# Attention and a maxout projection: token blocks by parity, 64x64 tiles for the last queries, transposes by DMA

## The chip, the cores and the metric

The kernel runs on one core of a Trainium2 chip. The metric is the device time of one execution in microseconds. The kernel before takes 380.43 us, the median of three runs (380.34 to 380.91). A profiled execution of it spans 377.6 us from its first to its last instruction.

Engines are named as in the profile: PE is TensorE (matmuls), PEld its weight loads, DVE is VectorE, ACT is ScalarE, POOL is GpSimd, SP is SyncE. PSUM is the memory that matmuls write, eight banks; one bank holds 512 fp32 columns on 128 partitions.

## The reference

Softmax attention with one added to the denominator, for 8 batches of 12 heads of 448 tokens and 64 dimensions, then a projection with the maximum of three matrices, then an output matrix. Inputs and output are fp32.

```python
# q, k, v: (8, 12, 448, 64)
scores = scale * np.matmul(q, k.transpose(0, 1, 3, 2))      # scale = 1 / sqrt(64)
m = np.max(scores, axis=-1, keepdims=True)
e = np.exp(scores - m)
attn = e / (np.sum(e, axis=-1, keepdims=True) + np.exp(-m) + 1e-09)
x = matmul(attn, v)                                         # heads side by side: (3584, 768)
h = np.maximum(np.maximum(x @ w1, x @ w2), x @ w3)          # w1, w2, w3: (768, 768)
out = h @ w_out                                             # (3584, 768)
```

Without the shift by the maximum the weight is exp(s) / (sum of exp(s) + 1), which is what both kernels compute, in fp16 with fp32 sums.

## The kernel before

The heads are taken in 24 groups of four (8 batches, three groups each). Tokens are split into 4 chunks of 112. A group has four visits; in each, scores of two chunks for a pair of heads go to PSUM, ScalarE takes exponentials, and between the visits TensorE works off pieces of the projections of the batch before. All loads cast from fp32 to fp16 and are issued by GpSimd.

```python
SC = 112; NCH = 4; GH = 4           # chunk, chunks, heads in a group
ps1 = tile_pool(bufs=4, PSUM)       # one bank each: transposes, sums, projections
ps2 = tile_pool(bufs=2, PSUM)       # two banks each: scores

# transpose_pair: per pair of heads, K and Q in 4 chunks each
nc.tensor.transpose(out=trT[:, n, ts(c, SC)], in_=t16[:, c, :, :], identity=ident16[0:SC, 0:SC])
nc.vector.tensor_copy(out=qkT, in_=trT.rearrange("p n s -> p (n s)"))

# scores_visit: keys of a chunk as rows, two heads in the two halves of the array
nc.tensor.matmul(out=stp[:, hh, 0:S], lhsT=qkT[hh*D : hh*D + D, c*SC : c*SC + 128],
                 rhs=qkT[hh*D : hh*D + D, S : 2*S], start=True, stop=True)
nc.scalar.activation(out=st["eT"][:, 2*pr : 2*pr + 2, c, :], in_=stp[0:SC, :, 0:S],
                     func=AF.Exp, scale=scale)

# av_group: three column-tiled sums, four heads in four strips of 32 columns
for c in range(NCH):
    for hh in range(GH):
        nc.tensor.matmul(out=bank[32*hh : 32*hh + 32, 0:S], lhsT=weights(hh, c),
                         rhs=eT[:, hh, c, :], start=(c == 0), stop=(c == NCH - 1))
# weights: ones (the denominator), then the even and the odd columns of V
nc.scalar.activation(out=lnd, in_=den[:, 0:S], func=AF.Ln, bias=one_b)
nc.scalar.activation(out=rb, in_=lnd, func=AF.Exp, bias=ln_lam, scale=-1.0)
nc.vector.tensor_tensor(out=xT[b][:, 2*g + hf, :], in0=num[:, 0:S], in1=rb, op=ALU.mult)

# up_piece: 6 matmuls of 448 columns, then a copy or a maximum into hT
# out_piece: 6 matmuls of 384 columns, scaled into o_sb; a stored tile has 768 columns
```

In the last steps, the sums of the last group are followed by all pieces of the last batch.

Of the kernel before, what the change touches and what calls it, by code (L numbers as in the profile page):

```python
# [21 lines left out]
def kernel(  # L22
# [16 lines left out]
    SC = 112  # L39
    NCH = S // SC  # L40
    NDC = DM // 128
    NFC = DFF // 128
    GH = 4
    NG = H // GH
    scale = 1.0 / math.sqrt(D)

    tabs = list(get_activation_tables(nc.m.arch).keys())
# [10 lines left out]
    cpool = ctx.enter_context(tc.tile_pool(name="const", bufs=1))  # L58
    ld_pool = ctx.enter_context(tc.tile_pool(name="ld", bufs=5))
    p16_pool = ctx.enter_context(tc.tile_pool(name="p16", bufs=2))  # L60
    att_pool = ctx.enter_context(tc.tile_pool(name="att", bufs=4))
    e_pool = ctx.enter_context(tc.tile_pool(name="e", bufs=2))
    small = ctx.enter_context(tc.tile_pool(name="small", bufs=2))
    xt_pool = ctx.enter_context(tc.tile_pool(name="xt", bufs=2))
    ht_pool = ctx.enter_context(tc.tile_pool(name="ht", bufs=2))
    out_pool = ctx.enter_context(tc.tile_pool(name="outp", bufs=3))

    ps1 = ctx.enter_context(tc.tile_pool(name="ps1", bufs=4, space=bass.MemoryType.PSUM))
    ps2 = ctx.enter_context(tc.tile_pool(name="ps2", bufs=2, space=bass.MemoryType.PSUM))

    ctx.enter_context(tc.manual_schedule())

    groups = [(b, g) for b in range(B) for g in range(NG)]
    raw = {}

    def load_group(i, which="qkv", step=GH):
        b, g = groups[i]
        tiles = raw.setdefault(i, {})
        for name in which:
            tiles[name] = ld_pool.tile(  # L80
                [SC, GH, NCH, D], MMDT, tag="ld_" + name, name="ld_" + name
            )
        for h0 in range(0, GH, step):
            for name in which:
                src = {"q": q, "k": k, "v": v}[name][b].rearrange(
                    "(g h) (p c) d -> g p h (c d)", g=NG, c=NCH
                )[g]
                nc.gpsimd.dma_start(  # L88
                    out=tiles[name][:, h0 : h0 + step].rearrange("p h c d -> p h (c d)"),
                    in_=src[:, h0 : h0 + step],  # L90
                )

    load_group(0, "qk", 2)
    ident16 = cpool.tile([128, 128], MMDT, name="ident16")
    make_identity(nc, ident16)
    load_group(1, "qk")
    load_group(0, "v")
    load_group(1, "v")
    load_group(2)
    ones16 = cpool.tile([SC, 32], MMDT, name="ones16")  # L100
    nc.vector.memset(ones16, 1.0)
    one_b = cpool.tile([128, 1], FP32, name="one_b")
    nc.vector.memset(one_b, 1.0)

    ln_lam = cpool.tile([128, 1], FP32, name="ln_lam")
    nc.vector.memset(ln_lam, math.log(LAMBDA))

    w_sb = [cpool.tile([128, NDC, DFF], MMDT, name=f"w{i}") for i in range(4)]
    wout_sb = w_sb[3]

    def load_weight(i):
        w = (moe_w1, moe_w2, moe_w3, moe_w_out)[i]
        for g in range(NG):
            if i < 3:
                src = w.rearrange("(g p hf) f -> g p hf f", g=NG, hf=2)[g]
            else:
                src = w.rearrange("(g hf p) f -> g p hf f", g=NG, hf=2)[g]
            nc.gpsimd.dma_start(out=w_sb[i][:, 2 * g : 2 * g + 2, :], in_=src)


    state = {}

    def pair_qk(i):
        qf, kf = raw[i].pop("q"), raw[i].pop("k")
        qk16 = []
        for pr in range(GH // 2):
            q16 = p16_pool.tile([SC, NCH, 2, D], MMDT, tag=f"q16_{pr}", name=f"q16_{pr}")
            k16 = p16_pool.tile([SC, NCH, 2, D], MMDT, tag=f"k16_{pr}", name=f"k16_{pr}")
            nc.vector.tensor_copy(
                out=k16, in_=kf[:, 2 * pr : 2 * pr + 2].rearrange("p h c d -> p c h d")  # L130
            )
            nc.vector.tensor_copy(
                out=q16, in_=qf[:, 2 * pr : 2 * pr + 2].rearrange("p h c d -> p c h d")
            )
            qk16.append((q16, k16))
        state[i] = {"qk16": qk16, "qkT": []}

    def transpose_pair(i, pr):
        st = state[i]
        q16, k16 = st["qk16"][pr]  # L140
        trT = ps1.tile([128, 2, S], MMDT, tag="bank1", name="trT")
        for n, t16 in enumerate((k16, q16)):
            for c in range(NCH):
                nc.tensor.transpose(  # L144
                    out=trT[:, n, ts(c, SC)], in_=t16[:, c, :, :],
                    identity=ident16[0:SC, 0:SC],
                )
        qkT = att_pool.tile([2 * D, 2 * S], MMDT, tag="qkT", name="qkT")
        nc.vector.tensor_copy(out=qkT, in_=trT.rearrange("p n s -> p (n s)"))  # L149
        st["qkT"].append(qkT)  # L150

    def scores_visit(i, pr, cs):
        st = state[i]
        if "eT" not in st:
            st["eT"] = e_pool.tile([SC, GH, NCH, S], MMDT, tag="eT", name="eT")
        qkT = st["qkT"][pr]
        stps = []
        for c in cs:
            stp = ps2.tile([128, 2, 512], FP32, tag="bank2", name="stp")
            for hh in range(2):  # L160
                nc.tensor.matmul(  # L161
                    out=stp[:, hh, 0:S],
                    lhsT=qkT[hh * D : hh * D + D, c * SC : c * SC + 128],
                    rhs=qkT[hh * D : hh * D + D, S : 2 * S],
                    start=True,
                    stop=True,
                )
            stps.append(stp)
        for c, stp in zip(cs, stps):
            nc.scalar.activation(  # L170
                out=st["eT"][:, 2 * pr : 2 * pr + 2, c, :],
                in_=stp[0:SC, :, 0:S],
                func=AF.Exp,
                scale=scale,
            )

    xT = {}

    def av_group(i):
        b, g = groups[i]  # L180
        st = state.pop(i)
        eT, v16 = st["eT"], raw[i].pop("v")
        if g == 0:
            xT[b] = xt_pool.tile([128, NDC, S], MMDT, tag="xT", name="xT")

        def col_tiled(weights):
            bank = ps1.tile([128, 512], FP32, tag="bank1", name="av")
            for c in range(NCH):
                for hh in range(GH):
                    nc.tensor.matmul(  # L190
                        out=bank[32 * hh : 32 * hh + 32, 0:S],
                        lhsT=weights(hh, c),
                        rhs=eT[:, hh, c, :],
                        start=(c == 0),
                        stop=(c == NCH - 1),
                    )
            return bank

        den = col_tiled(lambda hh, c: ones16[:, :])
        lnd = small.tile([128, S], FP32, tag="lnd", name="lnd")  # L200
        nc.scalar.activation(out=lnd, in_=den[:, 0:S], func=AF.Ln, bias=one_b)  # L201
        rb = small.tile([128, S], FP32, tag="rb", name="rb")
        nc.scalar.activation(out=rb, in_=lnd, func=AF.Exp, bias=ln_lam, scale=-1.0)  # L203
        for hf in range(2):
            num = col_tiled(lambda hh, c: v16[:, hh, c, hf::2])
            nc.vector.tensor_tensor(  # L206
                out=xT[b][:, 2 * g + hf, :], in0=num[:, 0:S], in1=rb, op=ALU.mult
            )

# [4 lines left out]
    def up_piece(b, fc, i):  # L214
        if b % 2 == 0 and fc == 0 and i == 0:
            hT[b // 2] = ht_pool.tile([128, NFC, 2 * S], MMDT, tag="hT", name="hT")
        dst = hT[b // 2][:, fc, (b % 2) * S : (b % 2) * S + S]
        p_i = ps1.tile([128, 512], FP32, tag="bank1", name="p_i")
        for dc in range(NDC):
            nc.tensor.matmul(  # L220
                out=p_i[:, 0:S],
                lhsT=w_sb[i][:, dc, ts(fc, 128)],
                rhs=xT[b][:, dc, :],
                start=(dc == 0),
                stop=(dc == NDC - 1),
            )
        if i == 0:
            nc.vector.tensor_copy(out=dst, in_=p_i[:, 0:S])  # L228
        else:
            nc.vector.tensor_tensor(out=dst, in0=dst, in1=p_i[:, 0:S], op=ALU.max)  # L230

    NH = 2
    NW = DM // NH

    def out_piece(bp, t, nh):
# [33 lines left out]
    def add_pieces(b):  # L269
        order = [(fc, i) for fc in range(NFC) for i in range(3)]  # L270
        if b == 0:
            order = [(fc, i) for i in range(3) for fc in range(NFC)]
# [98 lines left out]
```

The softmax here doesn't subtract the row's maximum and nothing guards it: scores larger than these inputs give would overflow.

## Time and profile before

| what | value |
|---|---|
| time, median of 3 | 380.43 us |
| span of the profiled execution | 377.6 us |
| granted TensorE clock, mean | 0.999 |
| `p_i` (up projection), share of the chain that ended last | 43.4% |
| `op_ps` (output projection) | 15.0% |
| `av` (sums) | 11.0% |
| `stp` (scores) | 10.0% |
| `trT` (transposes) | 4.2% |
| loads of weights, K and Q | 8.9% |

Busy time is given by engine, with the share of the span. Rows of 40 digits cut the span into 40 equal slices; a digit is the busy share in tenths. In a table by stage the columns are: the stage, its length, then busy time and number of instructions of PE, PEld, DVE, ACT and POOL, then the granted clock, the DMA share and GB/s. The chain that ended last is followed back from the last instruction, at each step to what released it. In a timeline, what stands in brackets is how long the engine was idle before, and what released it.

### The profile page before, as it was taken

The page shows a single profiled execution, that of the slowest core. Times are in us where ns is not written, and L with a number is a line of the kernel's source. Part 1 is how long each engine was busy: PE and PEld are TensorE (multiplying, and loading weights), DVE is VectorE, ACT ScalarE, POOL GpSimd, SP SyncE. Part 2 cuts the span into 40 slices and gives each one's busy share as a digit, 9 for nine tenths or more (in the row PEclk, how much of TensorE's full clock was granted, in tenths as well). Part 3 has the DMA queues.
Part 4 walks back from the last instruction along what each step waited for, and adds up shares of the span by engine and source line. Part 5 has one row for each costly group of instructions (what it writes and reads, how often), then busy time and mean ns, then how long its engine had stood idle before and what let it go on. Part 6 is the DMA issues. An engine that isn't in the chain of part 4 may idle for free.

```text
span 377.6 us, 7320 instructions
## 1 busy us (share of the span) xinstructions
PE 358.3 (95%) x3120; PEld 172.0 (46%) x3120; DVE 194.7 (52%) x395; ACT 194.5 (52%) x241; POOL 59.4 (16%) x92
## 2 busy tenths in 40 slices
PE   2777999999999999999999999999999999999995
PEld 1233444544445444454445544454444554445552
DVE  2233545545546546546546555455465465445553
ACT  1879464663655655555555645546555554552000
POOL 8533450220210201202202202202000000000000
PEclk9999999999999999999999999999999999999999
DMA  7999998555508625455236555077010410013005
GB/s 92 185 208 206 204 196 121 73 136 68 73 2 151 111 54 75 60 139 75 32 43 89 126 101 73 6 128 141 2 26 0 128 43 0 2 32 95 2 0 168
DMA packets 40064, 32.71 MB, mean 87 GB/s; under 512 B 2272, under 2 KB 35296, under 8 KB 40032
## 3 DMA queue, kind: packets, MB, share of 16 engines
q0 software_dynamic: 35552, 21.24, 40.8%
q1 hardware_dynamic: 4480, 11.01, 9.8%
q8 instruction: 24, 0.39, 0.5%
q14 instruction: 8, 0.07, 0.0%
HBM read 42.47 MB, written 11.01 MB: 142 GB/s over the span
## 4 chain that ended last, share of the span: by engine, by line
PE 84%; DMA 9%; ACT 2%; POOL 2%; DVE 1%; issue 1%; DVEq 0%; POOLq 0%
PE p_i L220 43%; PE op_ps L241 15%; PE av L190 11%; PE stp L161 10%; PE trT L144 4%; DMA w_123<-in_moe_w_dram 3%; DMA ld_k<-in_k_dram 3%; DMA ld_q<-in_q_dram 2%; DVE xT L206 1%; ACT eT L170 1%; ACT rb L203 1%; ACT lnd L201 1%; POOL ld_q L88 1%; POOL ld_k L88 1%; POOL ld_v L88 0%
## 5 line engine op out<-in xcount | busy, mean ns | idle before, releaser
L170 ACT ACTIVATE eT<-stp 112x896 f16<-112x896 f32 x192 | 164.9, 916 | 145.1 <-PE stp L161 145.1
L230 DVE TENSOR_TENSOR hT<-hT,p_i 128x448 f16<-128x448 f16 x96 | 59.4, 619 | 45.5 <-PE p_i L220 45.1
L206 DVE TENSOR_TENSOR xT<-av,rb 128x448 f16<-128x448 f32 x48 | 27.8, 619 | 70.8 <-ACT rb L203 64.7
L220 PE MATMUL p_i<-xT,w_122 128*128 128x448 f16 x288 | 63.0, 353 | 0.4
L220 PE MATMUL p_i<-xT,w_123 128*128 128x448 f16 x288 | 62.4, 353 | 0.0
L220 PE MATMUL p_i<-xT,w_124 128*128 128x448 f16 x288 | 62.2, 353 | 0.0
L161 PE MATMUL stp<-qkT 64*128 64x448 f16 x384 | 56.3, 364 | 4.9 <-ACT eT L170 4.8
L241 PE MATMUL op_ps<-w_125,hT 128*128 128x384 f16 x336 | 59.5, 326 | 0.0
L88 POOL DMA_DIRECT2D ld_v<-in_v_dram x24 | 16.8, 702 | 192.3 <-PE av L190 126.3
L248 DVE TENSOR_SCALAR o_sb<-op_ps 128x384 f32<-128x384 f32 x56 | 31.2, 557 | 28.5 <-PE op_ps L241 28.4
L241 PEld LDWEIGHTS <-hT 128*128 128x128 f16 x336 | 30.9, 98 | 24.8 <-issue 6.3
L190 PE MATMUL av<-eT,ld_v 112*32 112x448 f16 x768 | 41.8, 361 | 0.0
L228 DVE CAST hT<-p_i 128x448 f16<-128x448 f32 x48 | 29.7, 620 | 19.9 <-PE p_i L220 19.9
L220 PEld LDWEIGHTS <-w_123 128*128 128x128 f16 x288 | 25.9, 98 | 29.6 <-issue 9.2
L220 PEld LDWEIGHTS <-w_124 128*128 128x128 f16 x288 | 26.0, 98 | 28.7 <-issue 7.8
L220 PEld LDWEIGHTS <-w_122 128*128 128x128 f16 x288 | 26.1, 98 | 27.8 <-issue 7.0
L149 DVE COPY qkT<-trT 128x896 f16<-128x896 f16 x48 | 29.5, 615 | 3.1 <-PE trT L144 3.0
L161 PEld LDWEIGHTS <-qkT 64*128 64x128 f16 x384 | 12.0, 94 | 40.9 <-issue 40.3
L190 PEld LDWEIGHTS <-ld_v 112*32 112x32 f16 x768 | 21.0, 99 | 16.8 <-issue 1.7
L190 PE MATMUL av<-eT,ones_116 112*32 112x448 f16 x384 | 23.3, 364 | 0.0
L88 POOL DMA_DIRECT2D ld_q<-in_q_dram x25 | 17.7, 709 | 6.9 <-DMA w_124<-in_moe_w_dram 1.5
L88 POOL DMA_DIRECT2D ld_k<-in_k_dram x25 | 17.6, 703 | 4.4 <-DMA w_123<-in_moe_w_dram 1.1
(305 smaller groups left out, 142.1 us busy)
## 6 DMA issues: line engine op xcount, KB each, us to landing
ld_v<-in_v_dram POOLq DMA_DIRECT2D x24, 224.0 KB, 4.0
ld_q<-in_q_dram POOLq DMA_DIRECT2D x23, 224.0 KB, 4.9
ld_k<-in_k_dram POOLq DMA_DIRECT2D x23, 224.0 KB, 5.9
out_dram<-o_sb SPq DMA_DIRECT2D x8, 336.0 KB, 2.8
out_dram<-o_sb SPq DMA_DIRECT2D x8, 288.0 KB, 2.7
out_dram<-o_sb SPq DMA_DIRECT2D x8, 240.0 KB, 2.8
out_dram<-o_sb SPq DMA_DIRECT2D x8, 192.0 KB, 2.7
w_122<-in_moe_w_dram POOLq DMA_DIRECT2D x3, 384.0 KB, 10.7
```

Of the source, the lines that this page charges most:

```text
L88: nc.gpsimd.dma_start(out=tiles[name][:, h0 : h0 + step].rearrange("p h c d -> p h (c d)"), in_=src[:, h0 : h0 + step],)
L144: nc.tensor.transpose(out=trT[:, n, ts(c, SC)], in_=t16[:, c, :, :], identity=ident16[0:SC, 0:SC],)
L149: nc.vector.tensor_copy(out=qkT, in_=trT.rearrange("p n s -> p (n s)"))
L161: nc.tensor.matmul(out=stp[:, hh, 0:S], lhsT=qkT[hh * D : hh * D + D, c * SC : c * SC + 128], rhs=qkT[hh * D : hh * D + D, S : 2 * S], sta ...
L170: nc.scalar.activation(out=st["eT"][:, 2 * pr : 2 * pr + 2, c, :], in_=stp[0:SC, :, 0:S], func=AF.Exp, scale=scale,)
L190: nc.tensor.matmul(out=bank[32 * hh : 32 * hh + 32, 0:S], lhsT=weights(hh, c), rhs=eT[:, hh, c, :], start=(c == 0), stop=(c == NCH - 1),)
L206: nc.vector.tensor_tensor(out=xT[b][:, 2 * g + hf, :], in0=num[:, 0:S], in1=rb, op=ALU.mult)
L220: nc.tensor.matmul(out=p_i[:, 0:S], lhsT=w_sb[i][:, dc, ts(fc, 128)], rhs=xT[b][:, dc, :], start=(dc == 0), stop=(dc == NDC - 1),)
L228: nc.vector.tensor_copy(out=dst, in_=p_i[:, 0:S])
L230: nc.vector.tensor_tensor(out=dst, in0=dst, in1=p_i[:, 0:S], op=ALU.max)
L241: nc.tensor.matmul(out=op_ps[:, 0:NW], lhsT=hT[bp][:, fc, ts(t, 128)], rhs=wout_sb[:, fc, ts(nh, NW)], start=(fc == 0), stop=(fc == NFC - 1),)
L248: nc.vector.tensor_scalar(out=o_sb[:, ts(nh, NW)], in0=op_ps[:, 0:NW], scalar1=1.0 / LAMBDA, scalar2=None, op0=ALU.mult,)
```

## The change

It joins several changes.

- **Tokens in blocks of 64 by parity.** A partition now holds 7 tokens of a head, so the 448 tokens of a head are 7 blocks of 64, one for each residue. The transposed Q and K of two neighbouring tokens stand in the two halves of the partitions. The scores are 64x64 tiles, four at a time: two row halves (the parity), two column halves (two blocks of keys).
- **Sums turned round.** The exponentials are now the weights and V is what moves, with a 65th column of 1/256 that gives the denominator. The result has queries as rows; it is normalised on VectorE and then transposed for the projections.
- **The last 64 queries as 64x64 tiles from group 3 on.** Seven blocks are three pairs and one left over. Instead of whole matmuls in which half of the rows are empty, the last block is summed in four 64x64 tiles in two PSUM banks, whose halves are added afterwards.
- **Transposes by DMA.** From group 7 on Q and K, and from group 6 on the attention result, are transposed by DMA, not by TensorE. GpSimd copies Q into the half of the other parity.
- **A start in two parts.** The first pair of heads comes uncast over two hardware queues, TensorE runs matmuls on zeros while it waits, and groups 0 to 2 are done for the last 192 queries first, then for the first 256, with the projections of the 192 between.
- **PSUM.** Three tiles of two banks for scores and sums, two of one bank for projections and transposes.
- **The end.** The last output tile is stored as 640 and 128 columns, over two queues.

The core of the diff; cuts are marked.

```diff
-    SC = 112
-    NCH = S // SC
+    HP = 64
+    T = S // HP
+    NE, NO = 4 * HP, 3 * HP
...
+    PE_QK = 7
+    PE_X = 2
+    LAST = 3
...
-    ps1 = ctx.enter_context(tc.tile_pool(name="ps1", bufs=4, space=bass.MemoryType.PSUM))
-    ps2 = ctx.enter_context(tc.tile_pool(name="ps2", bufs=2, space=bass.MemoryType.PSUM))
+    ps_s = ctx.enter_context(tc.tile_pool(name="ps_s", bufs=3, space=bass.MemoryType.PSUM))
+    ps_b = ctx.enter_context(tc.tile_pool(name="ps_b", bufs=2, space=bass.MemoryType.PSUM))
...
+    for nm, src, eng in (("k", k, nc.sync), ("q", q, nc.scalar)):
+        first[nm] = cpool.tile([P, T, D], FP32, name="first_" + nm)
+        pair = src[0, 0:2].rearrange("h (x t) d -> (h x) (t d)", t=T)
+        eng.dma_start(out=first[nm].rearrange("x t d -> x (t d)"), in_=pair)
...
+    def transpose_dma(i):
...
+        for dst, nm, o in ((QT[i], "q", 4), (KT[i], "k", 0)):
+            nc.sync.dma_start_transpose(
+                out=dst[:, o * 128 : (o + T) * 128].rearrange("p (j x) -> p j x", x=P),
+                in_=raw[i][nm][:, 1 : NB + 1].rearrange("x t d -> x (t d)"),
+            )
...
+    def scores(i, ej, units, part="EO"):
...
+                        nc.tensor.matmul(
+                            out=stp[half * HP : half * HP + HP, par, j * qn : (j + 1) * qn],
+                            lhsT=k_block(i, pr, h2, x[half]),
+                            rhs=q_cols(i, pr, h2, par, part),
+                            start=True,
+                            stop=True,
+                        )
...
+    def av_tail(i, ej, pr, ws=(0, 1, 2, 3)):
...    # the seventh block of keys, as 64x64 tiles
+    def av_last(i, ej, pr):
...    # the seventh block of queries, as 64x64 tiles
+    def av_main(i, ej, pr, ws=(0, 1, 2, 3), last=False):
+        for hh in range(2):
+            for j, w in enumerate(ws):
+                for c, x in enumerate((X1, X3, X2)):
+                    o = e_col(where[pr, hh, x], w)
+                    nc.tensor.matmul(
+                        out=ps[:, hh, j * D1 : (j + 1) * D1],
+                        lhsT=eF[:, o : o + 128],
+                        rhs=vx[:, 2 * pr + hh, (x[0]), 0:D1],
+                        start=False,
+                        stop=(c == 2),
...
+        nc.vector.reciprocal(out=rb, in_=rb)
+        nc.vector.tensor_tensor(
+            out=xn[i][:, pr, ws[0] : ws[0] + nw].rearrange("p j h d -> p h j d"),
...
-        lnd = small.tile([128, S], FP32, tag="lnd", name="lnd")
-        nc.scalar.activation(out=lnd, in_=den[:, 0:S], func=AF.Ln, bias=one_b)
...
+    def av(i, ej, pr, part):
+        if i >= LAST:
+            av_tail(i, ej, pr, (0, 1, 2))
+            av_last(i, ej, pr)
+            return av_main(i, ej, pr, (0, 1, 2), True)
+        av_tail(i, ej, pr, PW[part])
+        av_main(i, ej, pr, PW[part])
...
+            cuts = [(0, NW, None), (NW, NW, (sy, sy))]
+            if b == B - 1 and t == 6:
+                cuts = [(0, NW, None), (NW, 256, (sy, sc)), (NW + 256, 128, (sy, sc))]
...
+    visits = ((0, 1), (2, 3), (4, 5, 6))
...
+            scores(i, ej, units)
...
+            if vi < 2:
+                finish = av(i - 1, pj, vi, "E" if first else "EO")
...
+            if finish:
+                one()
+                finish()
+            if vi == 1 and i > 3 * PE_X:
+                x_transpose_dma(i - 1)
...
+            fill(per)
```

## The prediction, made before the changed kernel ran

> **What bounds the kernel now.** I read the page first, then four stages of the span, then the chain that ended last within one stretch of steady work, then the end of the timeline. The page's first two parts:
>
> ```profile
> span 377.6 us, 7320 instructions
> PE 358.3 (95%) x3120; PEld 172.0 (46%) x3120; DVE 194.7 (52%) x395; ACT 194.5 (52%) x241; POOL 59.4 (16%) x92
> ...
> PE   2777999999999999999999999999999999999995
> ...
> ACT  1879464663655655555555645546555554552000
> ...
> DMA  7999998555508625455236555077010410013005
> ```
>
> TensorE is busy in every slice but the first four and the last; no other engine is above 52%. The busy time per stage (PE, PEld, DVE, ACT, POOL) says the same:
>
> ```profile
> 0.00:38.73 38.73, 24.91 (x260) 11.11 (x260) 10.96 (x31) 26.51 (x33) 20.29 (x36) 1.00 1.11 173
> 38.73:47.44 8.71, 8.39 (x63) 3.90 (x60) 5.79 (x13) 3.72 (x6) 3.88 (x6) 1.00 1.26 204
> 47.44:342.78 295.34, 294.97 (x2618) 141.30 (x2622) 161.19 (x324) 162.95 (x202) 35.27 (x51) 1.00 0.45 75
> ```
>
> From 47 to 343 us TensorE never stops, at the full clock (1.00). So time there is the sum of issue times on TensorE, and these I take from the chain, where each piece is the time until the next piece begins (start, length, what), and not from the mean of a matmul on the page (353 ns), in which pipelined matmuls overlap. One group of four heads:
>
> ```profile
> 196.47 0.48 PE stp L161 x4
> 196.95 2.38 PE av L190 x48
> 199.33 1.24 PE p_i L220 x6
> 200.57 0.48 PE stp L161 x4
> 201.06 1.24 PE p_i L220 x6
> 202.30 0.40 PE trT L144 x8
> 202.70 0.98 PE op_ps L241 x6
> 203.67 0.48 PE stp L161 x4
> 204.16 1.08 PE op_ps L241 x6
> ```
>
> What the reader is to see: six output matmuls of 384 columns behind a transpose take 0.98 us (162.5 ns each); the same six behind a score tile take 1.08. In the last batch the six up-projection matmuls of 448 columns start every 1.137 us, 189.5 ns each; behind `stp` or `av` they take 1.24. Two pairs of `stp` should be 2 x 189.5 = 379 ns and take 484. So every step from tiled matmuls to whole ones or back costs about 0.105 us. Eight transposes of 112 columns take 0.40: 49.5 ns each. The sums (`av`, 48 matmuls, four at a time) are 12 x 189.5 = 2.27 us plus one step.
>
> Check: a group needs 36 x 189.5 + 14 x 162.5 + 8 x 189.5 (score pairs) + 12 x 189.5 + 16 x 49.5 = 13.68 us, plus nine steps = 14.63. The sums of two neighbouring groups begin at 109.13, 123.76 and 138.12: 14.6 and 14.4. The model holds.
>
> The end: the last scaling on VectorE, after which only the store's flight to 377.6 us is left, 4.1 us behind it.
>
> ```profile
> 372.95 0.56 DVE L248 TENSOR_SCALAR o_sb<-op_ps 128x384 f32<-128x384 f32 x1 [0.42 <-PE op_ps L241]
> ```
>
> **What the Trainium skill says.** (1) "TensorE: Matmul & The Clock Gate", section "Back-to-back issue gap", gives N/2.4 + 2.5 ns for a warm matmul of N columns: 189.2 for 448, 162.5 for 384, 49.2 for 112. The trace agrees (189.5, 162.5, 49.5). The same section's 81 ns for a stream of 128-column matmuls with weight loads does not fit: here 112 columns with a new weight load each take 49.5, and I go by that. (2) "TensorEngine Tiling (Array Packing)", section "Key Properties": changing the tiling mode drains the engine. The trace agrees, 0.105 us each way. (3) The same page, section "PSUM Bottleneck": tiling speeds up TensorE and not the emptying of PSUM; the trace of before shows no such wait (4.8 us on `stp` in all, early). (4) "DMA: Bandwidth & Descriptors", section "Latency and other measured facts": about 261 GB/s for a transposing DMA. No transfer in this trace transposes.
>
> **The change part by part.** The counts are from the order of both built programs.
>
> *Up and out projections.* Before 864 x 189.5 = 163.7 us. After 756 of 448 columns, 108 of 256 (109.2 ns by the formula) and 108 of 192 (82.5): 143.3 + 11.8 + 8.9 = 164.0. Output 336 x 162.5 = 54.6 both times. **+0.3**.
>
> *Scores.* Before 384/2 x 189.5 = 36.4. After, 64x64 tiles, four at a time, keys in blocks of 64 so that no row of a 128-row tile is empty (112 of 128 before): 588/4 x 189.5 + 84/4 x 109.2 + 84/4 x 82.5 = 31.9. **-4.5**.
>
> *Sums with V.* Before 54.6 us, a third of it the denominator from `ones`. Now the exponentials are the weights and V with a column of constants moves, 65 columns: 900 whole matmuls and 1188 of 64x64. This is the step I know least. By the formula 65 columns are 29.6 ns; a matmul with its own load of 128 weights has been seen at 49.5 and not below. I choose 36 ns, and 45 ns for four 64x64 tiles: 900 x 36 + 297 x 45 = 32.4 + 13.4 = 45.8. **-8.8**.
>
> *Transposes.* Before 384 x 49.5 = 19.0. After, 119 for Q and K of groups 0 to 6 and 48 for the attention result of groups 0 to 5, 128 columns (55.8 ns): 9.3. The rest goes through DMA, three transfers of about 0.25 MB in a group, 0.72 MB in some 13 us; at the page's rate an estimate of 2.8 us, hidden, as DMA is 0.45 busy in the steady stage. **-9.7**.
>
> *Steps between modes.* Before 24 groups x 0.95 = 22.8. After, scores and the 64x64 sums stand in one tiled stretch; the order shows 82 stretches, two steps each: 82 x 0.21 = 17.2. **-5.6**.
>
> *ScalarE and VectorE.* 24 x 7 exponentials of 896 at 0.86 us (164.9/192) are 6.0 us a group for 6.9 before, and Ln and Exp of 448 columns (1.3 us a group) go; small copies come. VectorE loses qkT copies and the four K and Q copies and gains a normalisation of about 1 us per pair of heads. Both stay near half busy; nothing for the sum.
>
> *Start.* Up to 38.73 us TensorE issues only three groups' attention, 3 x (4 x 0.484 + 2.38 + 0.8) = 15.4 us, so 23 us are lost, to loads and to exponentials (ACT 26.5 busy of 38.7). The change loads the first pair of heads uncast over the hardware queues, scores only 192 of 448 queries in all three groups first, and up-projects these. Exponentials are then 3/7 of 3 x 6.0, some 8 us instead of 25. But the first weight stands behind 4.3 MB of Q, K and V: 6.7 MB with itself. The page's first slices moved 92 and 185 GB/s of 2-byte data, which is twice that read: 5.2 MB by 18.9 us, 9.2 MB by 28.3, so the weight is there at about 22 us and the second at 30. TensorE has about 10 us of work before 22 us; 12 lost, and 4 in the stretch up to the third weight. 16 for 23.3. **-7.3**.
>
> *End.* The last piece is 128 columns instead of 384: the scaling takes perhaps a third of 0.56, the store as long as before. **-0.7**.
>
> *New stall.* Projections now have two PSUM banks where four served all. In the pure projection stretch of the last batch VectorE ends with a bank about 0.13 us before TensorE would come round to it (0.62 us copy, 1.137 us per piece). Each normalisation that VectorE does between makes TensorE wait a little: 42 of them at 0.1 us. **+4**.
>
> Sum: 0.3 - 4.5 - 8.8 - 9.7 - 5.6 - 7.3 - 0.7 + 4 = -32.3, from 380.4 us: **348 us**.
>
> **The rivals.** *Weight loads bound the sums.* At 49.5 ns a matmul and 60 ns a round of tiles the sums cost 62.4 instead of 45.8 and the time is 365. For it: no matmul with its own weights below 49.5 ns in the trace. Against: that is what its 112 columns need anyway, so the load was hidden. *The sums run at the column rate.* 29.6 and 30 ns: 35.6 us, the time is 338. *PSUM's two banks become the bound.* If VectorE is late by 0.5 us at each of 63 visits, 31 instead of 4: 375. For it is the thin 0.13 us; against it, VectorE at 55%, and that the program puts a projection piece ahead of the late part of each normalisation. *Transfers come late.* If transposing DMAs or the GpSimd queue (copies and five issues of 0.7 us a group) need more than a group's 13 us, TensorE waits in each group; 2 us in 17 groups gives 382. Against: they are issued one to two groups ahead. *The start gains nothing*, as the same bytes come first: 355.
>
> **Range and chances.** The sums give -10 to +17, the start +-7, the banks -4 to +15, rarely all on one side; the removed transposes, mode steps and score columns (20 us) are counts times measured times and hardly in doubt. 334 to 362 should hold it 8 times in 10. Faster by over 2% (below 372.8) 0.96, within 2% 0.03, slower 0.01: only late transfers or banks at their worst reach there.
>
> **What would show it.** In the chain of the changed kernel, between two groups after group 7: about 13.0 us apart, with no transposes; `stp` x28 at 0.19 us per four; the `avp` pieces about 0.95 us per pair of heads (0.8 or 1.3 for the first two rivals). Among TensorE's waits, those on VectorE's `hT` or `o_sb` for the banks, 4 us in all; none on a transposing DMA. First `p_i` near 22 us. Wrong would be: TensorE below 90% busy in the steady stage, or its clock under 1.00.

## The result and the profile after

The changed kernel takes 341.09 us, the median of four runs (340.13 to 342.21), beside 380.38 us before: a ratio of 0.898, 95% interval 0.895 to 0.901. The prediction was 348 with 334 to 362. Its profiled execution spans 339.7 us, 37.9 less than before.

The page's first two parts of the changed kernel:

```profile
span 339.7 us, 10313 instructions
PE 327.5 (96%) x4340; PEld 196.0 (58%) x4340; DVE 201.4 (59%) x539; ACT 187.8 (55%) x307; POOL 146.4 (43%) x260
...
PE   7899999999999999999999999999999999999993
...
DMA  8999999299697999969996889989991640114016
```

TensorE still bounds the kernel, and it is busy at 90% or more from the third slice on, where it was the fifth. GpSimd went from 16% to 43% (87 us more, 46.7 of them copies of Q), and the DMA engines are busy to the end of the steady part (the transposes), but nothing waits there for long. A stage of steady work, columns as before:

```profile
100.00:200.00 100.00, 100.00 (x1327) 56.27 (x1329) 60.99 (x165) 62.54 (x107) 46.96 (x85) 1.00 1.02 160
```

The chain that ended last, in one group of the changed kernel (start, length, what):

```profile
191.85 0.50 PE stp L304 x8
192.36 0.09 PE avp L344 x12
192.45 0.13 PE avp L361 x14
192.58 0.67 PE avp L388 x18
...
196.59 3.41 PE p_i L490 x18
199.99 0.69 PE stp L304 x12
200.69 3.51 PE p_i L490 x18
```

What is left out are twelve output matmuls and a second visit like the first; no transposes are left in the chain. Eight score tiles take 0.50 us: two rounds of four at 189.5 ns and one step. Eighteen up-projection matmuls take 3.51 us behind scores, and 3.41 behind the sums; the step between the modes then lies between the 64x64 sums (L344, L361) and the whole ones (L388), so 0.67 us is a step and 18 x 31.4 ns. The 26 tiles in 0.22 us are 34 ns for four. From group 11 to group 20 the first scores move from 128.12 to 242.03 us, 12.66 us a group; in the kernel before, the same groups took 14.67 (152.26 to 284.29 us).

The end: the last scaling is short, but the store behind it ends 4.8 us after it (4.1 before).

```profile
334.59 0.29 DVE o_sb L521
```

### The profile page after: what moved, and what is told of

It is laid out like the page before. It is cut to its first block, busy times and chain, and to the rows that moved or that the text cites. A ratio compares the mean times of both kernels' runs of the same rounds, so it can differ in the third digit from the quotient of the medians.

```text
span 339.7 us, 10313 instructions
## 1 busy us (share of the span) xinstructions
PE 327.5 (96%) x4340; PEld 196.0 (58%) x4340; DVE 201.4 (59%) x539; ACT 187.8 (55%) x307; POOL 146.4 (43%) x260
## 4 chain that ended last, share of the span: by engine, by line
PE 90%; DVE 4%; ACT 4%; issue 1%; ACTq 0%
PE p_i L490 49%; PE op_ps L514 15%; PE stp L304 11%; PE avp L388 9%; ACT e L324 3%; PE avp L344 2%; PE avp L361 2%; PE warm L175 1%; DVE xn L404 1%; DVE QT L190 1%; DVE hT L501 1%; PE trT L213 1%; DVE rb L401 0%; PE xtp L450 0%; PE trT L229 0%
## 5 line engine op out<-in xcount | busy, mean ns | idle before, releaser
L490 PE MATMUL p_i<-xT,w 128*128 128x448 f16 (+2 forms) x972 | 173.4, 332 | 2.0 <-DVE hT L501 1.0
L324 ACT ACTIVATE e<-stp 128x896 f16<-128x896 f32 (+4 forms) x171 | 143.5, 900 | 49.5 <-PE stp L304 49.1
L490 PEld LDWEIGHTS <-w 128*128 128x128 f16 x972 | 90.1, 98 | 71.2 <-issue 8.0
L249 POOL COPY QT<-QT 64x384 f16<-64x384 f16 (+1 forms) x84 | 46.7, 556 | 96.4 <-DMA QT<-ld_q 60.7
L501 DVE TENSOR_TENSOR hT<-hT,p_i 128x448 f16<-128x448 f16 (+2 forms) x96 | 59.7, 621 | 36.9 <-PE p_i L490 36.8
L514 PE MATMUL op_ps<-w,hT 128*128 128x384 f16 (+2 forms) x342 | 58.7, 323 | 0.0
L304 PE MATMUL stp<-QT,KT 64*64 64x448 f16 (+2 forms) x756 | 48.7, 340 | 2.3 <-ACT e L324 0.9
L521 DVE TENSOR_SCALAR o_sb<-op_ps 128x384 f32<-128x384 f32 (+2 forms) x57 | 31.2, 547 | 16.5 <-PE op_ps L514 15.9
L388 PE MATMUL avp<-vx,e 128*128 128x65 f16 x900 | 37.5, 194 | 0.0
L388 PEld LDWEIGHTS <-e 128*128 128x128 f16 x900 | 30.9, 97 | 2.3
L344 PEld LDWEIGHTS <-e 64*64 64x64 f16 x600 | 13.5, 107 | 9.1 <-issue 2.9
```

The source lines that it names most:

```text
L249: eng.tensor_copy(out=t[d0 : d0 + HP, o * 128 : (o + n) * 128], in_=t[s0 : s0 + HP, a * 128 : (a + n) * 128],)
L304: nc.tensor.matmul(out=stp[half * HP : half * HP + HP, par, j * qn : (j + 1) * qn], lhsT=k_block(i, pr, h2, x[half]), rhs=q_cols(i, pr, h2 ...
L324: nc.scalar.activation(out=dst, in_=src, func=AF.Exp, scale=scale)
L388: nc.tensor.matmul(out=ps[:, hh, j * D1 : (j + 1) * D1], lhsT=eF[:, o : o + 128], rhs=vx[:, 2 * pr + hh, (x[0]), 0:D1], start=False, stop= ...
L490: nc.tensor.matmul(out=p_i[:, j * qn : (j + 1) * qn], lhsT=w_sb[i][:, dc, ts(fc, 128)], rhs=xT[b][:, dc, q0 : q0 + qn], start=(dc == 0), s ...
L501: nc.vector.tensor_tensor(out=dst, in0=dst, in1=src, op=ALU.max)
```

## The experiments

Theory: the time is the sum of TensorE's issue times and of what it loses at the start and the end; each part of the change is worth the matmuls, the transposes and the mode steps that it takes away. Rivals: weight loads bound the sums; the two PSUM banks of the projections are the limit; most of the gain is the start.

Short diffs; "+" is the experiment. Times are medians, ratios are to the kernel before.

### The disputed cost by itself: the whole sums twice

```diff
-                for c, x in enumerate((X1, X3, X2)):
+                for c, x in enumerate((X1, X3, X2, X1, X3, X2)):
...
-                        stop=(c == 2),
+                        stop=(c == 5),
```

The output is of sums in which all but the seventh block of keys counts twice (the last 64 queries, which go through the tiles from group 3 on, keep their sums there).

> The 900 whole matmuls of 65 columns of the sums are done twice (the output is then of doubled sums), which measures the disputed cost by itself. The trace of the changed kernel has 18 of them in 0.67 us with one mode step of 0.105: 31.4 ns each, so +28 us, 369 us. The prediction's 36 ns would give +32 (373); a bound by the load of 128 weights, 49.5 ns, +45 (386).

Measured: 369.3 us, ratio 0.976 (0.969 to 0.982), which is 28.2 more than the changed kernel. In its chain:

```profile
195.47 1.23 PE avp L388 x36
```

36 take 1.23 us where 18 took 0.67: 31.1 ns each. The total says the same, 28.2 us / 900 = 31.3 ns, though its interval is some 5 us wide. A matmul of 65 columns with a new load of 128 x 128 weights costs its columns and hardly more. The bound by weight loads is out.

### One part alone in the kernel before: DMA transposes

```diff
+        if i >= 3:
+            qkT = att_pool.tile([2 * D, 2 * S], MMDT, tag="qkT", name="qkT")
+            for n, t16 in enumerate((k16, q16)):
+                nc.sync.dma_start_transpose(
+                    out=qkT[:, n * S : n * S + S].rearrange("p (c x) -> p c x", x=SC),
+                    in_=t16.rearrange("p c h d -> p (c h d)"),
+                )
...
```

> One part of the change alone, in the kernel before: Q and K of groups 3 to 23 are transposed by DMA (two transfers per pair of heads), which takes 336 of its 384 TensorE transposes of 49.5 ns and 42 copies out of PSUM away. Theory (parts add up): 380.4 - 16.6 = 364 us. Rival (the part pays only together with the others, or the transfers come late): above 372.

Measured: 372.5 us, ratio 0.981 (0.978 to 0.984): above the 372 of the rival, and less than half of the gain of the theory. The chain in the start:

```profile
33.51 8.34 DMA qkT<-q
...
41.98 0.93 PE stp L170 x4
42.91 4.60 PE av L199 x48
```

The first transposes, of group 3, are issued while the weights still fill the DMA engines, and TensorE waits 6.7 us for one that takes 8.3. Behind the wait it runs at half rate for a while: four scores in 0.93 us, not 0.48, 48 sums in 4.60, not 2.38. In the steady part the theory holds: the same visit two batches later (175.64 and 258.78 us) gives 13.86 us a group, 0.77 less than before, for 16 x 49.5 ns = 0.79. The sums of group 3 begin 7.6 us later than in the kernel before (58.92, not 51.36), those of the last group 7.1 us earlier (334.70, not 341.83). So the part is worth its count, and half was lost because it began too early.

### The same mistake in the changed kernel: DMA transposes earlier

```diff
-    PE_QK = 7
+    PE_QK = 5
-    PE_X = 2
+    PE_X = 1
```

> DMA transposes from group 5 on for Q and K and from group 3 on for the attention result, instead of 7 and 6: 52 TensorE transposes of 55.8 ns fewer (2.9 us), and 7 copies out of the projections' two banks. Theory (sum): 338 us; with the banks as the limit it is more, 335. Rival (loads of the weights still fill the DMA engines up to 60 us, so the transposes come late): slower than 341, with TensorE waiting on transposing DMAs.

Measured: 345.3 us, the median of four executions (two more, at 348.8 and 349.2 us, count as a slower state), ratio 0.908 (0.904 to 0.913). The rival holds. Its chain:

```profile
45.90 12.76 DMA KT<-ld_k
...
58.70 0.96 PE stp L304 x8
```

A transpose of group 5 needs 12.8 us (the median of this kernel is 5.6 for K), the scores wait 5.3 us for it, and behind the wait eight score tiles take 0.96 us instead of 0.50. The 2.9 us of fewer transposes are lost and 4 more. So groups 7 and 6 as first ones are no arbitrary choice; later ones were not tried.

### All transposes back on TensorE

```diff
-    PE_QK = 7
+    PE_QK = NI
-    PE_X = 2
+    PE_X = B
```

> The changed kernel with every transpose but the last group's back on TensorE (238 more for Q and K, 136 more for the attention result, 374 x 55.8 ns = 20.9 us). Theory (time is the sum of TensorE's issue times): 341 + 21 = 362 us, TensorE waits as few as now. Rival (the projections' two PSUM banks are the limit): every transpose tile takes one of them and a copy of 0.6 to 0.9 us on VectorE or ScalarE, some 51 more tiles; then 370 us or more, with waits of TensorE on those copies. Rival (transposes were hidden): under 350.

Measured: 389.3 us, ratio 1.026 (1.022 to 1.029), slower than the kernel before. TensorE's waits (who waited for whom, us in total, times, longest):

```profile
PE p_i L490 <- ACT QT L188: 8.4, 11, 0.8
PE p_i L490 <- DVE hT L499: 7.5, 23, 0.4
PE op_ps L514 <- DVE o_sb L521: 4.5, 13, 0.6
```

In the changed kernel such waits on hT are 1.4 us in all. The list begins a wait at the end of the last matmul, which is later than the moment at which the next could have been issued (353 ns after its start and not 189.5). Counted from the start of one matmul to the start of the next, less its issue time as measured above, the 64 listed waits of this kernel take 37.0 us, the 15 of the changed kernel 8.4: 28.6 more. With 20.9 of issue time that is 49.5, and the spans differ by 49.0 (388.7 and 339.7). The rival is right here: with two banks there is no room for transposes.

### The same transposes in the other banks

```diff
-        tp = ps_b.tile([128, 1024], MMDT, tag="b", name="trT")
+        tp = ps_s.tile([128, 2, 1024], MMDT, tag="s", name="trT")[:, 0]
```

and the same for the transposes of the attention result.

> The kernel with all transposes on TensorE (389 us), but they go to the three two-bank tiles of scores and sums instead of the two one-bank tiles of the projections. The same instructions otherwise. If the 27 us that it cost beyond its issue times come from the projections' two banks: 362 to 368 us, and TensorE's waits on copies of QT, hT and o_sb (22 us) nearly gone. If they come from VectorE and ScalarE being busy with the copies, or scores and sums now wait instead: 380 or more.

Measured: 377.4 us, ratio 0.994 (0.993 to 0.996). The waits on QT, hT and o_sb by the projections are gone, as expected, but others stand in their place:

```profile
PE xtp L465 <- ACT e L324: 12.9, 20, 0.7
PE avp L344 <- ACT QT L188: 4.3, 6, 0.9
```

Counted from start to start, waits take 21.8 us more than in the changed kernel. With 20.9 of issue time that is 42.7; 6.8 less is lost outside the waits (24 changes between tiled and whole matmuls now fall into a wait, not 3, which would hide their steps). Together 35.9, for 35.4 between the spans (375.1 and 339.7). So it is not the projections' two banks alone, as I had put it: all eight banks are in use, and a transpose takes one, in either pool, until ScalarE or VectorE has emptied it behind the exponentials.

### The start

Groups 0 to 2 for all queries at once, the projections of batch 0 after them:

```diff
-    attend("O", 0, S01)
-    ...
-    attend("E", 2, S46)
-    ...
+    for u in visits:
+        scores(0, 1, u)
+    ...
+    for i in (1, 2):
+        for vi, u in enumerate(visits):
+            scores(i, (i + 1) % NEB, u)
+            if vi < 2:
+                av(i - 1, i % NEB, vi, "EO")
```

> Groups 0 to 2 are done for all 448 queries at once, with loads, first pair and warm-up as in the changed kernel; the projections of batch 0 begin after them, in group 3. Ten tiled stretches fewer (-2.1 us). Theory (the start gains by giving TensorE projections before the exponentials of three groups are done): first up-projection near 33 us instead of 22.6, about 10 us more idle, 349 to 351 us. Rival (the weights' arrival bounds the start in any order): 339 to 342.

Measured: 343.5 us, ratio 0.904 (0.902 to 0.906). Neither: the first up-projection is later by 17 us (39.5, not 22.8), and the time by only 2.5. Both kernels begin group 4 at 43 to 44 us; the changed kernel, then this one:

```profile
43.74 0.50 PE stp L304 x8
43.07 0.50 PE stp L304 x8
```

The changed kernel has by then issued 72 up-projection matmuls of 192 columns and 20 of 256, 8.1 us of work; this one 18 of 448, 3.4 us. Less the 0.7 us by which it begins group 4 later, it is 4.0 us ahead; nine of its ten more tiled stretches lie before this point, so their cost is in this already. Of the 4.0 the time keeps 2.5. From 60 to 80 us TensorE is busy for 18.96 us in the changed kernel and for 19.64 in this one; the rest of the loss is not traced.

The weights' arrival does not bound the start either. The chain up to group 4 is TensorE for 27.5 us, VectorE for 7.3, ScalarE for 6.5 and no load in the changed kernel; here it is TensorE for 20.0, VectorE for 10.5, a first load for 4.3 and ScalarE for 3.4. In the kernel before, loads were 30.9 of the first 38.7 us. So the loads left the chain in either order of the groups.

### Scores and sums apart

```diff
+            if vi < 2 and i > 3:
+                one()
             if vi < 2:
                 finish = av(i - 1, pj, vi, "E" if first else "EO")
```

> A piece of the projections is put between the scores and the sums of a visit, so that they stand in two tiled stretches: 115 stretches for 82, by the order of instructions. The work is the same. Theory (a step costs 0.105 us each way): 33 x 0.21 = +6.9 us, 348 us. Rival (the step is only the drain of a long matmul and would be paid anyway): within 1 us of 341.

Measured: 361.5 us, ratio 0.952 (0.948 to 0.955): 20.4 more than the changed kernel, three times what was expected. The steps are there; in its chain:

```profile
260.80 0.50 PE stp L304 x8
261.30 1.24 PE p_i L490 x6
262.54 0.22 PE avp L344 x12
```

Six up-projection matmuls take 1.24 us (1.137 without a step), and the first tiles 0.22, not 0.09. But the later sums also hold their PSUM longer, and the next ones wait:

```profile
PE avp L344 <- DVE end L417: 6.1, 6, 1.2
```

And around one stretch in which TensorE kept waiting, its granted clock is lower (third column from the end of the stage table), and 18 up-projection matmuls take 5.35 us, not 3.41 (the chain):

```profile
80.00:86.00 6.00, 4.57 (x58) 2.56 (x59) 1.54 (x4) 4.42 (x7) 1.49 (x3) 0.61 1.31 186
84.34 5.35 PE p_i L490 x18
```

Counted from start to start, as for the transposes, waits take 12.8 us more than in the changed kernel, and 9.1 us more are lost outside them. Of these, 2.4 belong to the slow stretch (1.94 there, and 0.43 for 18 sums in 1.10 us, not 0.67). That leaves 6.7 us for the 33 more stretches, for which 6.9 were expected. So a step costs what was said; what had been left out is that keeping scores and sums apart makes TensorE wait as well.

### The last 64 queries

The changed kernel again, for the small differences of this and the next section:

> The changed kernel itself once more, on the chip of the three runs beside it, so that differences of one to four us can be read: 341 us, ratio 0.897 to 0.898.

Measured: 340.99 us, ratio 0.897 (0.894 to 0.900). Then whole matmuls for these queries, and tiles only from group 6 on:

```diff
-    LAST = 3
+    LAST = NI
```

(The calls of `finish` at the end, which then has nothing to do, are gone too.)

> The last 64 queries of groups 3 to 23 are summed by whole matmuls with half of the rows empty, as in groups 0 to 2: 252 more whole matmuls (31.4 ns), 420 fewer 64x64 tiles (34 ns for four). Theory (sum of issue times): +7.9 - 3.6 = +4.3 us, 345 us. Rival (the tiles' halves have to be added and scaled by small VectorE and ScalarE work, which costs as much as the tiles save): 341 or less. A third (two PSUM banks: with less small work on VectorE fewer waits): between the two.

Measured: 341.6 us, ratio 0.8985 (0.896 to 0.901), no difference that can be measured. TensorE does pay: its chain has 0.12 + 0.86 = 0.98 us for the sums of a pair of heads, the tiles 0.89, so 42 x 0.09 = 3.8 us. The listed waits on hT (1.4 us) disappear with the tiles' additions and scalings, and those on exponentials shrink by 0.7; counted from start to start, waits take 3.7 us less (4.7, not 8.4). The tiles were bought with about as much waiting as they save.

```diff
-    LAST = 3
+    LAST = 6
```

> The 64x64 tiles for the last 64 queries from group 6 on instead of group 3: groups 3 to 5, in which ScalarE and VectorE still have the copies of the transposes, are summed by whole matmuls. TensorE: 6 x 0.09 = +0.5 us. If the waits that the tiles' small work causes lie in these groups (1.4 us on hT and some on exponentials, gone in the kernel with whole sums throughout): 339 to 340 us, the fastest. If they lie all over the span: 341 to 341.5.

Measured: 338.9 us, ratio 0.891 (0.887 to 0.895), the lowest median of all. The listed waits on hT are gone, and the gain is there when the scores of group 5 begin, in the changed kernel and then in this one:

```profile
56.87 0.50 PE stp L304 x8
54.82 0.34 PE stp L304 x4
```

That fits, but its interval just meets that of the changed kernel (0.894 to 0.900), so 2 us is a likely gain and not a settled one.

### The end and the warm-up

The last tile stored like the others:

```diff
-            if b == B - 1 and t == 6:
-                cuts = [(0, NW, None), (NW, 256, (sy, sc)), (NW + 256, 128, (sy, sc))]
```

> The last output tile is computed and stored as 384 and 384 columns like the others, by one queue. The prediction gave the cut 0.7 us, so 341.8. From the trace of the changed kernel, in which 5.1 us lie between the start of the last scaling and the end where there were 4.65 before, the rival: no difference, or up to 0.5 us faster.

Measured: 341.3 us, ratio 0.898 (0.895 to 0.901). The cut is worth nothing that can be measured. And no matmuls on zeros:

```diff
-    warm(8)
...
-    warm(4)
```

> Both runs of matmuls on zeros in the start left out. In the changed kernel the first transposes, after 3.6 us of them, still go at half rate (about 107 ns), and from 9.9 us on at the full rate. Theory: without them the half rate lasts longer, some 60 transposes and small score tiles more at twice their time on a path that the exponentials share: +0.5 to +2 us, 342 us. Rival (the start is bound by loads and exponentials): no difference.

Measured: 342.8 us, ratio 0.904 (0.900 to 0.908); the first up-projection starts at 23.8 us, 1.0 and 1.2 later than in the two traces of the changed kernel. That is as expected, but its interval just meets that of the changed kernel (0.894 to 0.900).

## Why the prediction was right, step by step

| step | predicted, us | measured, us | from |
|---|---|---|---|
| up and out projections | +0.3 | +0.3 | 18 in 3.41 us |
| scores | -4.5 | -4.5 | 8 in 0.50 us |
| sums with V | -8.8 | -16.2 | 900 x 31.4 ns + 297 x 34 ns = 38.4 us |
| transposes | -9.7 | -9.5 | 122 and 48, not 119 and 48 |
| steps between modes | -5.6 | -5.6 | 3.51 behind scores, 3.41 else |
| idle: start, end, banks | -7.3 - 0.7 + 4 = -4.0 | -2.4 | rest of the spans |
| sum | -32.3 | -37.9 | spans |

TensorE's issue times add up to 351.1 us before and 315.6 after; 26.5 and 24.1 us of the spans are left. The rows of steps and of both projections are counts times measured times; no run changed them alone in the kernel before. The medians differ by 39.3 us, 1.4 more than the two spans: the kernel before has spans from 376.7 to 380.1 us in later executions, and the one profiled, with 377.6, is among the short ones.

**Right.** That TensorE's issue times bound the kernel before and after, and that the gain is their difference: 35.5 of 37.9 us. The first up-projection was expected near 22 us and starts at 22.8; by then the first weight has landed (21.3 us), and what it waits for last is the attention result, so the hit owes something to chance. A group was expected to take 13.0 us and takes 12.66. No transposing DMA was to hold TensorE up: none does in the list of its waits, and a second trace of the changed kernel has one wait of 1.2 us, on the attention result. The estimate of 2.8 us for the three transfers of a group was far off as a duration: 5.3, 5.7 and 4.0 us from issue to landing (medians); they were issued early enough for that not to matter.

**Mis-sized: the sums.** "I choose 36 ns, and 45 ns for four 64x64 tiles" was too high; they are 31.3 and 34. This term alone is 7.4 us, and the prediction was 6.9 above the measured time. It was the rival "the sums run at the column rate". The Trainium skill's N/2.4 + 2.5 ns ("TensorE: Matmul & The Clock Gate", "Back-to-back issue gap") gives 29.6 for 65 columns, and the measured 31.3 is close; I leaned on the 49.5 ns of the transposes, which was no bound: 112 columns need that time themselves. The same section's 81 ns for a stream of 128-column matmuls with weight loads is not what these streams do: seven transposes of 128 columns take 0.39 us, 55.8 ns each.

**Mis-sized, and nearly cancelling: start and banks.** Start, end and banks together were to take 4.0 us less than the idle of before, and took 2.4 less. Listed waits on the projections' banks are 1.4 us, not 4: VectorE keeps up. The end gains nothing: 5.1 us lie behind the start of the last scaling, 4.65 before. By difference the start takes 4.2 us less, not 7.3, and its order in two parts brings 2.5: TensorE's first projections come 17 us earlier, but group 4 begins no earlier. The loads did leave the chain, as the prediction meant them to; TensorE, VectorE and ScalarE together then set the pace.

**Right for a narrower reason than given: transposes.** The sum priced them at 9.5 us. That holds from the kernel before, where 336 transposes fewer gave 0.77 us a group for 0.79. Inside the changed kernel 374 transposes cost 48 us for 20.9 of issue time, since its eight PSUM banks are taken. The prediction did name "PSUM's two banks become the bound" as a rival, and the change escapes it because the transposes have left. The Trainium skill's warning that emptying PSUM may become the limit once tiling has made TensorE faster ("TensorEngine Tiling (Array Packing)", "PSUM Bottleneck") fits the two runs with transposes on TensorE, which wait 28.6 and 21.8 us more; the changed kernel itself hardly waits.

What stays open: where 1.5 of the 4.0 us that the two-part start is ahead go, and whether tiles from group 6 on are really faster. Of the parts, only the DMA transposes were tried alone in the kernel before; what the turned sums would bring there is argued from the sum.

## What to carry to other kernels

Where one engine never stops, add up its issue times from the chain, mode steps included; of 37.9 us saved, 35.5 are the difference of two such sums, once the new matmul is measured. A part's price holds only while the buffers around it have room: a transpose was worth its issue time with the old PSUM layout and more than twice that with the new one. Transposing DMAs that start while weights are loading cost half of what they saved later in one kernel here, and more than they saved in the other, so begin after that.

## What the runs showed that I had not expected

- A matmul of 65 columns with its own 128 x 128 weights issues every 31.3 ns, and four 64x64 tiles of 65 columns in 34 ns.
- A transposing DMA of 224 KB takes 5.3 to 5.7 us to land in the steady part (medians for Q and K), and 12.8 us once while weights were loading.
- Behind a wait of 6.7 us in one kernel and 5.3 in another, TensorE goes at half rate (48 sums in 4.60 us, not 2.38; eight score tiles in 0.96, not 0.50), so such a wait costs more than its length. In the first, 36 sums shortly before the wait were slow already (3.20 us), so the wait is not the only cause.
- TensorE also starts at half rate, and the clock column does not show it. In the kernel before, the first 16 sums with `ones` take 1.69 us, those of the next group 0.94:

```profile
17.67 1.69 PE L190 MATMUL av<-eT,ones_116 112*32 112x448 f16 x16
27.82 0.94 PE L190 MATMUL av<-eT,ones_116 112*32 112x448 f16 x16
```

In the changed kernel, even after 3.6 us of matmuls on zeros, the first seven transposes take 0.76 us (109 ns each, not 55.8):

```profile
1.20 3.60 PE warm L175 x8
4.79 0.76 PE trT L213 x7
```

The clock entries in these traces begin only at 21.9 and at 7.1 us, and the page counts the time before as full. So the clock of 1.00 in the first stage of the kernel before is no measurement up to 21.9 us; part of the 23 us that the prediction put down to loads and exponentials is half rate. The chain there holds loads only, so what the half rate cost is not shown.
